# A fused attention and MLP kernel: two heads per load in the first batches, weight requests moved by a slot, small operations moved from VectorE to GpSimd, four more units kept for the end, the last tile in two halves

## The chip, the core and the metric

The kernel runs on one core of a Trainium2 chip. The core has a matrix engine (TensorE, PE in the profile, its weight loads PEld), VectorE (DVE), ScalarE (ACT), GpSimd (POOL) and a fifth engine, SyncE (SP), which here only issues DMA transfers. Each engine runs its instructions in the order in which they are written and waits on semaphores for the others. The metric is the device time in microseconds (us), taken as the median of several runs.

## What is computed

For 8 batches of 8 heads, with 576 positions and 64 dimensions per head, a causal attention with a position bias taken from a running sum of `s`, followed by a layer norm, an MLP of 512 to 2048 to 512 with a relu, and a residual. In short:

```python
scores = scale * q @ k.T                       # per head, 576 x 576
cum = cumsum(max(s, 0))
scores = where(causal, -1e9, scores + min(-(cum[:, None] - cum[None, :]), 0))
attn = softmax(scores)
x = concat_heads(attn @ v)                     # 8 x 576 x 512
xn = (x - mean(x)) / sqrt(var(x) + 1e-6) * g_ln
out = x + relu(xn @ w_ch1) @ w_ch2
```

All inputs and the output are float32 in HBM. The matmuls run in bfloat16.

## The kernel before

**Slots.** The 64 heads are numbered g = 8 * batch + head. The main loop (L714 to L739) has one slot for each. In slot g the score matmuls of head g are issued (`score_mms`), then their exps on ScalarE, then the products with v of head g - 1 (`values`, which ends with a reciprocal and a multiplication into x on VectorE). Around these stand hooks: `at(g, pos, f)` puts a piece of other work at place "a", "a2", "b", "x", "c", "d" or "e" of slot g. The code is scheduled by hand: what is written first is issued first on its engine.

**The bias.** Each head's q and k are extended by four columns with the running sum in three bfloat16 pieces, so that the score matmul adds the bias. `split` (L515 to L522) makes the three pieces with four operations. It runs for batch 0 in the prologue, for batch 1 in slot 2 and for batches 2 to 7 in slot 12. `shift` (L144 to L147) writes the pieces of one batch into the tile `aug` with two operations. `aug` holds q and k of one batch in bfloat16, 128 partitions by 5 row tiles by 16 by 128 columns; the columns from 68 on are padding, which only the DMA transposes of batches 3 and later read. For batches 0 to 2, q and k are transposed by TensorE (`t_quads`, four row tiles and a tail per matrix, copied out of PSUM by VectorE or ScalarE).

**Loads of batches 0 to 2.** These go per head: `head_in` (L422) issues one DMA of 128 KB for a head of q, k or v (512 rows of 64 floats), `tails_in` (L415) one for the last 64 rows of several heads. q and k arrive with four consecutive rows per partition. They land in homes that are reused: k of batch 1 lands where q of batch 0 was, q of batch 2 where k of batch 1 was, and so on, so that a load waits until GpSimd, VectorE or ScalarE have cast the old data to bfloat16 (`cast_head`, from `feed(g)` in slot g for head g + 4). SP issues all of them: batch 0 in the prologue (L460 to L467), batch 1 at the ends of slots 1 and 3, batch 2 in slots 12, 13 and 14 (three, three and two heads). A DMA waits on one of eight semaphores that are used in turn, so SP can have eight transfers under way.

**Weights.** The two weight matrices are requested by GpSimd, which also converts them to bfloat16 on the way: four requests for the up weights (`load_w1`) in slots 7, 7, 8, 8 and four for the down weights (`load_w2`) in slots 9, 9, 10, 10. The first up matmuls stand in slot 11.

**Units.** The MLP of a batch is cut into 32 units of four matmuls each over 512 columns (`chunk_units`: `up` with a relu on ScalarE or VectorE, `down` in quarters, whose last quarter ends with an eviction `yo` on VectorE and a store). The last 64 rows of the batches are gathered in pairs into four further tiles, worked on in two tail chunks of two tiles each, the second of which is the last work of the kernel. The list `units` is worked off inside the slots of the next batch, `nu` units per slot, until KEEP = 10 are left; those are for the end of the batch, where `last_of(b)` computes the last head's values, the layer norm statistics, the normalised `xn` and its transpose, the latter by a DMA for the later batches. Between these steps it works off units. After the loop, the remaining units run one after the other, and their stores are issued by SP.

**Start.** While the first loads are under way, TensorE runs 11 matmuls on the identity matrix whose result nobody reads (`spin(11)`, L493), then the transposes of the running sum (`pq`), which wait for the scan on VectorE. VectorE and GpSimd write a number of constants first (L468 to L481), among them the zero rows under the tails of q, k and v in their homes, and the padding of `aug`: row tile 0 by VectorE, row tiles 1 to 4 by GpSimd at the ends of slots 7 to 10.

Of the kernel before, what the change touches and what calls it, by code (L numbers as in the profile page):

```python
# [9 lines left out]
F32 = mybir.dt.float32  # L10
BF16 = mybir.dt.bfloat16
ALU = mybir.AluOpType
# [4 lines left out]
def kernel(  # L17
# [11 lines left out]
    nc = tc.nc  # L29

    B, H, S, D = q.shape
# [93 lines left out]
    def copy(eng, o, i):  # L125
        if eng == "act":
            nc.scalar.copy(out=o, in_=i)
        elif eng == "dve":
            nc.vector.tensor_copy(out=o, in_=i)  # L129
        else:  # L130
            nc.gpsimd.tensor_copy(out=o, in_=i)  # L131
# [24 lines left out]


    qkT = {}

    def new_t(b):  # L160
        qkT[b] = tpool.tile([P, HD, SP_], BF16, name="qkT", tag="qkT")
# [3 lines left out]
    def t_quads(b, h, engs):  # L165
        pts = [ps_m.tile([P, 2 * 512], BF16, name="pt", tag="pm") for _ in range(2)]
        tails = pts[1][0:DK, NF * P : NF * P + 2 * P].rearrange("r (j n) -> r j n", j=2)
        for i in range(2):
            for p in range(NF):
                nc.tensor.transpose(  # L170
                    pts[i][0:DK, p * P : (p + 1) * P], aug[:, p, i * H + h, 0:DK], ident
                )
# [6 lines left out]
        copy(  # L179
            engs[2],  # L180
            qkT[b][0:DK, :, NF * P : S].rearrange("r (j h) n -> r j h n", j=2)[:, :, h, :],
            tails[:, :, 0:TL],
        )

    def t_dma(b, p):
        nc.sync.dma_start_transpose(
# [168 lines left out]
    def chunk_units(c):  # L355
        st = {}
        na = 2 if c >= B else 4
        per = 4 // na
        tok = na * P

        def up(u):
            if u == 0:
                st["h"] = hpool.tile([P, FB, tok], BF16, name="hT", tag="hT")
            ph = ps_m.tile([P, 512], F32, name="ph", tag="pm")
            for j in range(per):
                fb = u * per + j
                for kd in range(KD):
                    nc.tensor.matmul(  # L368
                        ph[:, j * tok : (j + 1) * tok], lhsT=w1_bf[:, kd, fb * P : (fb + 1) * P],
                        rhs=xnT[c][:, :, kd, :], start=(kd == 0), stop=(kd == KD - 1),  # L370
                    )
            o = st["h"][:, u * per : (u + 1) * per, :].rearrange("p f t -> p (f t)")
            relu(u, o, ph)

        def down(a, qr):
            if qr == 0:
                st["py"] = ps_m.tile([P, 512], F32, name="py", tag="pm")
            for fb in range(4 * qr, 4 * qr + 4):
                nc.tensor.matmul(  # L379
                    st["py"], lhsT=st["h"][:, fb, a * P : (a + 1) * P], rhs=w2_bf[:, fb, :],  # L380
                    start=(fb == 0), stop=(fb == FB - 1),
                )
            if qr == 3:
                yo = ypool.tile([P, Dm], F32, name="yo", tag="yo")
                nc.vector.scalar_tensor_tensor(  # L385
                    out=yo, in0=st["py"], scalar=rstds[c][:, a : a + 1], in1=x_of(c, a),
                    op0=ALU.mult, op1=ALU.add,
                )
                store(c, a, yo)

        for u in range(FB // per):
            units.append(lambda u=u: up(u))
        for a in range(na):
            for qr in range(4):
                units.append(lambda a=a, qr=qr: down(a, qr))

    def mlp(n, eng=None):
        for _ in range(min(n, len(units))):
            stores(eng or nc.scalar, 0 if eng else 1)
            units.pop(0)()  # L400
# [18 lines left out]
            in_=src[what][b, hs, NF * P : S, :].rearrange("h s d -> s h d"),  # L419
        )  # L420

    def head_in(what, b, h, eng):  # L422
        o, i = homes[what, b][:, h, 0:NF, :], src[what][b, h, 0 : NF * P, :]
        if b in QUADS and what != "v":
            eng.dma_start(  # L425
                out=o.rearrange("p t d -> p (t d)"), in_=i.rearrange("(p t) d -> p (t d)", t=NF)
            )
        else:
            eng.dma_start(out=o, in_=i.rearrange("(t p) d -> p t d", p=P))  # L429

    def cast_head(what, b, h, eng):
        i = homes[what, b][:, h, :, :]
# [82 lines left out]
    def split(lo, hi, eng, a=None, o=None):  # L515
        r = r8[:, :, lo:hi]
        a = c8[:, :, lo:hi] if a is None else a
        o = cumh[:, :, lo:hi, :] if o is None else o
        eng.tensor_copy(out=o[:, :, :, 0], in_=a)
        eng.tensor_tensor(out=r, in0=a, in1=o[:, :, :, 0], op=ALU.subtract)  # L520
        eng.tensor_copy(out=o[:, :, :, 1], in_=r)
        eng.tensor_tensor(out=o[:, :, :, 2], in0=r, in1=o[:, :, :, 1], op=ALU.subtract)  # L522
# [36 lines left out]
    def at(g, pos, f):  # L559
        hooks.setdefault((g, pos), []).append(f)  # L560
# [13 lines left out]
    def t_next(g):  # L574
        t_quads(
            (g + 2) // H, (g + 2) % H,
            ("act" if g in(9,10) else "dve", "act" if g >= H else "dve", "dve"),
        )
# [16 lines left out]
    def heads_in(b, hs):  # L595
        for h in hs:
            for what in "qkv":
                head_in(what, b, h, nc.sync)

    def b1_in(h):  # L600
        heads_in(1, (h,))
# [112 lines left out]
    for g in range(NG + 4):  # L714

        nu = n_units.get(g, 0 if g < H else 4)
        if 2 * H <= g < NG:
            nu = max(0, -((KEEP - len(units)) // (H - g % H)))
        run(g, "a")
        if g >= 3:  # L720
            loads()
        if g < NG:
            score_tail = score_mms(g)
            run(g, "a2")
            score_tail()
            score_exp(g, 0)
        mlp(min(1, nu))
# [44 lines left out]
```

The softmax here doesn't subtract the row's maximum and nothing guards it: scores larger than these inputs give would overflow.

## Time and profile before

| | |
|---|---|
| median of 11 runs | 373.03 us (371.65 to 374.45) |
| the profiled execution | 373.2 us |
| its span, first to last instruction | 371.4 us |
| granted TensorE clock, mean | 0.997 |
| HBM read / written | 36.85 MB / 9.44 MB |

The profile is of one execution. It lists the busy time of each engine, the time from the start of the span at which each instruction ran, what an engine had waited for when it started after a pause (in brackets, with the pause in us), and the chain of work that ended last. L numbers are lines of the kernel before. Matmuls are pipelined: a matmul of 512 columns is shown as 379 ns, but 8 of them in a row take 1.73 us. Some matmul records are missing, which shows as short pauses in their place. Where each engine's time is summed over a stretch, the five pairs of numbers are busy us and instructions of PE, PEld, DVE, ACT and POOL; then come the granted TensorE clock, the mean busy share of the 16 DMA engines (it can be above 1, where packets overlap) and GB/s.

The DMA engines are busy for nine tenths or more in most slices of the first 90 us and less than half as much near the end. In the first 75 us the loads of the first three batches and all weights arrive: the eight weight requests are at 28.16, 28.95, 32.11, 32.84, 39.65, 40.47, 46.84 and 47.65 us.

### The profile page before, as it was taken

What the parts mean: (1) busy time and instruction counts of PE and PEld (TensorE: products, weight loads), DVE (VectorE), ACT (ScalarE), POOL (GpSimd) and SP (SyncE); (2) the same over time, 40 slices, a digit from 0 to 9 for tenths busy, and PEclk for the clock granted to TensorE, in tenths of its full rate; (3) what the DMA queues carried; (4) which work ended last, traced back from release to release, by engine and by line L of the source; (5) the groups of instructions that cost most, each with busy time, mean ns of one, the idle gap of its engine ahead of it and who ended that gap; (6) DMA issues with size and microseconds to landing.
All of it is one profiled execution on the core that took longest, in us unless ns stands there. A gap on an engine that the chain in (4) does not pass through costs nothing.

```text
span 371.4 us, 7843 instructions
## 1 busy us (share of the span) xinstructions
PE 351.4 (95%) x2955; PEld 200.6 (54%) x2981; DVE 202.7 (55%) x472; ACT 164.7 (44%) x298; POOL 168.7 (45%) x331
## 2 busy tenths in 40 slices
PE   6997989898999999999999999999999999899994
PEld 2876655564554555555556655455555555344471
DVE  6899585754457345674447335823563454933231
ACT  2767854354542566246524446335634562031020
POOL 5669764855445445484446534654443112500000
PEclk9999999999999999999999999999999999999998
DMA  8979999995998599989999999599404001520202
GB/s 184 232 196 187 215 206 234 230 243 124 208 213 216 131 201 213 224 167 217 196 251 186 222 243 199 76 246 201 100 33 110 31 2 56 116 56 0 86 28 56
DMA packets 168997, 58.86 MB, mean 158 GB/s; under 512 B 154048, under 2 KB 164288, under 8 KB 168960
## 3 DMA queue, kind: packets, MB, share of 16 engines
q1 hardware_dynamic: 158912, 46.17, 62.1%
q0 software_dynamic: 4256, 4.20, 6.8%
q10 hardware_dynamic: 5792, 8.00, 6.7%
q8 instruction: 23, 0.38, 0.4%
q14 instruction: 14, 0.11, 0.1%
HBM read 36.85 MB, written 9.44 MB: 125 GB/s over the span
## 4 chain that ended last, share of the span: by engine, by line
PE 71%; DVE 6%; DMA 3%; SPq 3%; POOL 2%; issue 1%; DVEq 0%; POOLq 0%
PE ph L368 30%; PE py L379 27%; PE s L207 8%; PE pot L258 6%; DVE xn L318 1%; DMA ring<-in_q_dram 1%; POOL aug L131 1%; DMA xnT<-xn 1%; DVE stats L303 1%; SPq L120 1%; SPq L425 1%; DMA x<-in_v_dram 1%; DVE x L267 1%; DVE yo L385 1%; SPq L429 0%
## 5 line engine op out<-in xcount | busy, mean ns | idle before, releaser
L227 ACT ACTIVATE e<-s 128x1024 bf16<-128x1024 f32 (+1 forms) x128 | 99.1, 808 | 85.3 <-PE s L207 85.3
L379 PE MATMUL py<-w_bf,hT 128*128 128x512 bf16 x550 | 129.8, 379 | 1.4
L368 PE MATMUL ph<-xnT,w_bf 128*128 128x512 bf16 x512 | 120.7, 379 | 1.9 <-DMA xnT<-xn 1.8
L230 POOL TENSOR_SCALAR_AFFINE_SELECT e<-e 128x384 bf16<-128x384 bf16 x104 | 45.7, 464 | 111.3 <-ACT e L227 102.7
L353 DVE TENSOR_SCALAR hT<-ph 128x512 bf16<-128x512 f32 x72 | 49.6, 691 | 76.5 <-PE ph L368 75.9
L368 PEld LDWEIGHTS <-w_bf 128*128 128x128 bf16 x640 | 58.2, 98 | 50.5 <-DMA xnT<-xn 2.3
L379 PEld LDWEIGHTS <-hT 128*128 128x128 bf16 x576 | 53.1, 98 | 56.0
L351 ACT ACTIVATE hT<-ph 128x512 bf16<-128x512 f32 x72 | 43.0, 597 | 79.3 <-PE ph L368 78.7
L207 PE MATMUL s<-qkT 68*128 68x192 bf16 (+5 forms) x368 | 55.4, 277 | 0.8 <-DVE qkT L129 0.8
L207 PEld LDWEIGHTS <-qkT 68*128 68x128 bf16 x432 | 36.8, 97 | 31.0 <-DVE x L267 3.0
L385 DVE SCALAR_TENSOR_TENSOR yo<-py,rstd,x 128x512 f32<-128x512 f32 x32 | 24.0, 749 | 47.6 <-PE py L379 45.4
L131 POOL CAST aug<-ring 128x512 bf16<-128x512 f32 (+2 forms) x85 | 44.7, 553 | 6.6 <-DMA ring<-in_k_dram 3.7
L258 PEld LDWEIGHTS <-e 128*128 128x128 bf16 x960 | 37.1, 98 | 12.4 <-POOL e L230 0.8
L258 PE MATMUL pot<-v_bf,e 128*128 128x65 bf16 x960 | 39.7, 193 | 0.6 <-POOL e L230 0.6
L267 DVE TENSOR_TENSOR x<-pot,rinv 128x320 f32<-128x320 f32 x64 | 31.5, 492 | 2.5 <-DMA ring<-in_q_dram 0.2
L129 DVE COPY qkT<-pt 68x512 bf16<-68x512 bf16 (+1 forms) x54 | 24.2, 482 | 8.5 <-PE pt L170 5.0
L303 DVE BATCH_NORM_STATS2 stats<-x 128x6 f32<-128x256 f32 (+2 forms) x68 | 23.4, 399 | 0.3
L318 DVE SCALAR_TENSOR_TENSOR xn<-x,mv,gln_b 128x512 bf16<-128x512 f32 x32 | 22.6, 748 | 0.0
L131 POOL CAST v_bf<-ring 128x512 bf16<-128x512 f32 (+2 forms) x33 | 18.2, 575 | 3.8 <-DMA ring<-in_v_dram 3.8
L266 DVE RECIPROCAL rinv<-pot 128x5 f32<-128x5 f32 x64 | 12.0, 187 | 14.6 <-PE pot L258 14.4
L324 POOL TENSOR_TENSOR rstd<-rstd,nhalf 128x2 f32<-128x2 f32 x18 | 18.9, 1052 | 1.5
L170 PE MATMUL pt<-ident,aug 128*68 128x128 bf16 x192 | 16.4, 219 | 2.9 <-DVE qkT L129 1.4
(78 smaller groups left out, 200.2 us busy)
## 6 DMA issues: line engine op xcount, KB each, us to landing
out_dram<-yo ACTq DMA_DIRECT2D x27, 256.0 KB, 3.4
ring<-in_q_dram SPq DMA_DIRECT2D x20, 256.0 KB, 4.3
ring<-in_k_dram SPq DMA_DIRECT2D x20, 256.0 KB, 4.9
ring<-in_v_dram SPq DMA_DIRECT2D x20, 256.0 KB, 4.2
w_bf<-in_moe_w_ch_dram POOLq DMA_DIRECT2D x8, 512.0 KB, 10.2
ring<-in_k_dram SPq DMA_DIRECT2D x30, 128.0 KB, 3.2
ring<-in_q_dram SPq DMA_DIRECT2D x22, 128.0 KB, 4.0
x<-in_v_dram SPq DMA_DIRECT2D x17, 128.0 KB, 3.6
```

Of the source, the lines that this page charges most:

```text
L131: nc.gpsimd.tensor_copy(out=o, in_=i)
L207: nc.tensor.matmul(d, lhsT=lhsT, rhs=qkT[b][0:DK, h, c0:c1], start=True, stop=not m)
L227: nc.scalar.activation(out=o, in_=i, func=ACT.Exp, scale=scale)
L230: nc.gpsimd.affine_select(out=d, in_=d, compare_op=ALU.is_ge, fill=0.0, base=0, pattern=[[0, d.shape[1]], [1, P]], channel_multiplier=-1,)
L258: nc.tensor.matmul(pot[:, t * D1 : (t + 1) * D1], lhsT=e[:, c : c + P], rhs=v_bfs[b % 2][:, kb, h, :], start=(kb == 0), stop=(kb == t),)
L267: nc.vector.tensor_tensor(out=xs[b][:, :, h * D : (h + 1) * D], in0=pv[:, :, 0:D], in1=rv.to_broadcast([P, NT, D]), op=ALU.mult,)
L303: nc.vector.bn_stats(out=sts[c, a][:, part, :], in_=x_of(c, a)[:, lo:hi])
L351: nc.scalar.activation(out=o, in_=i, func=ACT.Relu)
L353: nc.vector.tensor_scalar_max(out=o, in0=i, scalar1=0.0)
L368: nc.tensor.matmul(ph[:, j * tok : (j + 1) * tok], lhsT=w1_bf[:, kd, fb * P : (fb + 1) * P], rhs=xnT[c][:, :, kd, :], start=(kd == 0), sto ...
L379: nc.tensor.matmul(st["py"], lhsT=st["h"][:, fb, a * P : (a + 1) * P], rhs=w2_bf[:, fb, :], start=(fb == 0), stop=(fb == FB - 1),)
L385: nc.vector.scalar_tensor_tensor(out=yo, in0=st["py"], scalar=rstds[c][:, a : a + 1], in1=x_of(c, a), op0=ALU.mult, op1=ALU.add,)
```

## The change

- `head_in` gets a count `n`. For q and k it loads n heads with one DMA; for v it still issues one DMA per head. In batch 0 heads 0 and 1 are loaded one by one and the rest in pairs. Batches 1 and 2 are loaded in pairs: batch 1 still in slots 1 and 3, batch 2 in slots 11 to 14, one pair in each, where it was slots 12 to 14.
- The two calls of `split` in slots 2 and 12 and the `shift` of batch 1 in slot 5 go from VectorE to GpSimd.
- `load_w1` is called in slots 8, 8, 9, 9.
- The zero rows of v's home of batch 0 are written by VectorE instead of GpSimd, those of q's home of batch 1 by GpSimd in slot 1 instead of before the first loads. The padding of row tile 0 of `aug` is written by GpSimd instead of VectorE; the five GpSimd writes are at the ends of slots 7 to 11.
- `spin(11)` becomes `spin(9)`.
- In the last batch's slots 14 units are kept instead of 10.
- The last tile's 16 down matmuls of 512 columns become two groups of 16 with 256 columns, in two PSUM tiles, each with its own eviction. Each half is stored by two DMAs, one issued by SP and one by ScalarE.
- `t_quads` gets a way to put its third copy behind an exp ("act later"), which no call uses.

```diff
-    def head_in(what, b, h, eng):
-        o, i = homes[what, b][:, h, 0:NF, :], src[what][b, h, 0 : NF * P, :]
-        if b in QUADS and what != "v":
+    def head_in(what, b, h, eng, n=1):
+        if what != "v":
             eng.dma_start(
-                out=o.rearrange("p t d -> p (t d)"), in_=i.rearrange("(p t) d -> p (t d)", t=NF)
+                out=homes[what, b][:, h : h + n, 0:NF, :].rearrange("p h t d -> p h (t d)"),
+                in_=src[what][b, h : h + n, 0 : NF * P, :].rearrange("h (p t) d -> p h (t d)", t=NF),
             )
...
-    for h in range(H + 1):
-        if h < H:
-            head_in("q", 0, h, nc.sync)
-            head_in("k", 0, h, nc.sync)
-        if h:
-            head_in("v", 0, h - 1, nc.sync)
+    for h in (0, 1):
+        for what in "qk":
+            head_in(what, 0, h, nc.sync)
+    head_in("v", 0, 0, nc.sync, 1)
+    for h in range(2, H, 2):
+        for what in "qk":
+            head_in(what, 0, h, nc.sync, 2)
+        head_in("v", 0, h - 1, nc.sync, 2)
+    head_in("v", 0, H - 1, nc.sync)
...
-    for what, eng in zip("qkv", (nc.vector, nc.vector, nc.gpsimd)):
-        eng.memset(homes[what, 0][TL:P, :, NF, :], 0.0)
-    nc.gpsimd.memset(homes["q", 1][TL:P, :, NF, :], 0.0)
-    nc.vector.memset(aug[:, 0, :, DK:P], 0.0)
+    for what in "qkv":
+        nc.vector.memset(homes[what, 0][TL:P, :, NF, :], 0.0)
...
-    spin(11)
+    spin(9)
...
-    at(2, "c", lambda: split(H, 2 * H, nc.vector))
-    at(12, "c", lambda: split(2 * H, BH, nc.vector))
-    at(5, "b", lambda: shift(1, nc.vector))
+    at(2, "c", lambda: split(H, 2 * H, nc.gpsimd))
+    at(12, "c", lambda: split(2 * H, BH, nc.gpsimd))
+    at(5, "b", lambda: shift(1, nc.gpsimd))
...
-    for c, g in enumerate((7, 7, 8, 8)):
+    for c, g in enumerate((8,8,9,9)):
         at(g, "a", lambda c=c: load_w1(c))
...
-    for h, g in enumerate((1, 1, 1, 1, 3, 3, 3, 3)):
+    for h, g in zip(range(0, H, 2), (1, 1, 3, 3)):
         at(g, "e", lambda h=h: b1_in(h))
...
-    for p in (1, 2, 3, 4):
-        at(6 + p, "e", lambda p=p: nc.gpsimd.memset(aug[:, p, :, DK:P], 0.0))
-    B2 = 12
+    at(1, "b", lambda: nc.gpsimd.memset(homes["q", 1][TL:P, :, NF, :], 0.0))
+    for p in range(NT):
+        at(7 + p, "e", lambda p=p: nc.gpsimd.memset(aug[:, p, :, DK:P], 0.0))
+    B2 = 11
...
-        heads_in(2, range(3 * (g - B2), min(H, 3 * (g - B2) + 3)))
-    for g in (B2, B2 + 1, B2 + 2):
+        heads_in(2, 2 * (g - B2))
+    for g in range(B2, B2 + HH):
         at(g, "a", lambda g=g: b2_in(g))
...
-            nu = max(0, -((KEEP - len(units)) // (H - g % H)))
+            keep = 14 if g >= NG - H else KEEP
+            nu = max(0, -((keep - len(units)) // (H - g % H)))
```

The function for the last tile, called in place of the last `down` of the second tail chunk:

```python
def last(a):
    yo = ypool.tile([P, Dm], F32, name="yo", tag="yo")
    for j, (lo, hi) in enumerate(((0, 256), (256, Dm))):
        py = st["py"] if j == 0 else ps_m.tile([P, 512], F32, name="py", tag="pm")
        for fb in range(FB):
            nc.tensor.matmul(
                py[:, lo:hi], lhsT=st["h"][:, fb, a * P : (a + 1) * P],
                rhs=w2_bf[:, fb, lo:hi], start=(fb == 0), stop=(fb == FB - 1),
            )
        nc.vector.scalar_tensor_tensor(
            out=yo[:, lo:hi], in0=py[:, lo:hi], scalar=rstds[c][:, a : a + 1],
            in1=x_of(c, a)[:, lo:hi], op0=ALU.mult, op1=ALU.add,
        )
        for i, eng in enumerate((nc.sync, nc.scalar)):
            eng.dma_start(
                out=out[B - 2 + i, NF * P : S, lo:hi], in_=yo[i * TL : (i + 1) * TL, lo:hi]
            )
```

More of the change, by code (lines that the diff above doesn't have):

```diff
@@ L158 @@
     qkT = {}
+    behind_exp = []
     def new_t(b):
@@ L178, in t_quads @@
             )
[L179 to L183, printed above, removed]
+        o = qkT[b][0:DK, :, NF * P : S].rearrange("r (j h) n -> r j h n", j=2)[:, :, h, :]
+        if engs[2] == "act later":
+            behind_exp.append(
+                lambda: [copy("act", o[:, i, :], tails[:, i, 0:TL]) for i in range(2)]
+            )
+        else:
+            copy(engs[2], o, tails[:, :, 0:TL])
     def t_dma(b, p):
@@ L373, in up @@
             relu(u, o, ph)
+        def last(a):
+            yo = ypool.tile([P, Dm], F32, name="yo", tag="yo")
+            for j, (lo, hi) in enumerate(((0, 256), (256, Dm))):
+                py = st["py"] if j == 0 else ps_m.tile([P, 512], F32, name="py", tag="pm")
+                for fb in range(FB):
+                    nc.tensor.matmul(
+                        py[:, lo:hi], lhsT=st["h"][:, fb, a * P : (a + 1) * P],
+                        rhs=w2_bf[:, fb, lo:hi], start=(fb == 0), stop=(fb == FB - 1),
+                    )
+                nc.vector.scalar_tensor_tensor(
+                    out=yo[:, lo:hi], in0=py[:, lo:hi], scalar=rstds[c][:, a : a + 1],
+                    in1=x_of(c, a)[:, lo:hi], op0=ALU.mult, op1=ALU.add,
+                )
+                for i, eng in enumerate((nc.sync, nc.scalar)):
+                    eng.dma_start(
+                        out=out[B - 2 + i, NF * P : S, lo:hi], in_=yo[i * TL : (i + 1) * TL, lo:hi]
+                    )
         def down(a, qr):
@@ L377, in down @@
                 st["py"] = ps_m.tile([P, 512], F32, name="py", tag="pm")
+            if (c, a) == (B + 1, 1):
+                return last(a) if qr == 3 else None
             for fb in range(4 * qr, 4 * qr + 4):
@@ L420, in tails_in @@
         )
-    def head_in(what, b, h, eng):
-        o, i = homes[what, b][:, h, 0:NF, :], src[what][b, h, 0 : NF * P, :]
-        if b in QUADS and what != "v":
+    def head_in(what, b, h, eng, n=1):
+        if what != "v":
             eng.dma_start(
-                out=o.rearrange("p t d -> p (t d)"), in_=i.rearrange("(p t) d -> p (t d)", t=NF)
-            )
-        else:
-            eng.dma_start(out=o, in_=i.rearrange("(t p) d -> p t d", p=P))
+                out=homes[what, b][:, h : h + n, 0:NF, :].rearrange("p h t d -> p h (t d)"),
+                in_=src[what][b, h : h + n, 0 : NF * P, :].rearrange("h (p t) d -> p h (t d)", t=NF),
+            )
+        else:
+            for j in range(h, h + n):
+                eng.dma_start(
+                    out=homes[what, b][:, j, 0:NF, :],
+                    in_=v[b, j, 0 : NF * P, :].rearrange("(t p) d -> p t d", p=P),
+                )
     def cast_head(what, b, h, eng):
@@ L576, in t_next @@
             (g + 2) // H, (g + 2) % H,
-            ("act" if g in(9,10) else "dve", "act" if g >= H else "dve", "dve"),
+            (
+                "act" if g in (9, 10) else "dve",
+                "act" if g >= H else "dve",
+                "dve",
+            ),
         )
@@ L591, with heads_in @@
             at(g, "a2" if g < H else "b", lambda g=g: t_next(g))
-    for c, g in enumerate((7, 7, 8, 8)):
+    for c, g in enumerate((8,8,9,9)):
         at(g, "a", lambda c=c: load_w1(c))
[L595 to L598, printed above, removed]
+    def heads_in(b, h):
+        for what in "qkv":
+            head_in(what, b, h, nc.sync, 2)
     def b1_in(h):
-        heads_in(1, (h,))
+        heads_in(1, h)
         if h % HH == 0:
@@ L726 @@
             score_exp(g, 0)
+            while behind_exp:
+                behind_exp.pop(0)()
         mlp(min(1, nu))
```

## The prediction

> **What bounds the kernel now.** I read the page's busy table first, then the stretches, then the chain of waits, and last the order of time of the engines wherever the chain leaves TensorE.
>
> ```profile
> PE 351.4 (95%) x2955; PEld 200.6 (54%) x2981; DVE 202.7 (55%) x472; ACT 164.7 (44%) x298; POOL 168.7 (45%) x331
> ```
>
> ```profile
> 15.00:40.00 25.00, 21.86 (x387) 18.85 (x385) 23.56 (x69) 18.79 (x36) 19.39 (x37) 1.00 0.92 196
> 40.00:54.00 14.00, 12.40 (x129) 7.58 (x127) 8.58 (x19) 9.22 (x17) 9.99 (x19) 1.00 1.21 212
> ```
>
> TensorE is busy for 95% of the span, so nothing done on another engine counts unless TensorE stands still for it. The columns of the stretches are PE, PEld, DVE, ACT, POOL. From 15 to 40 us VectorE is busy 23.56 of 25.00: there it is the bound. From 40 to 54 us TensorE loses 1.60 us and the DMA engines are full (1.21). These rows of TensorE's order of time show who stops it (the idle is counted from the modelled end of the matmul before; from issue to issue each hole is some 0.16 longer):
>
> ```profile
> 29.35 0.20 PE L207 MATMUL pot<-qkT 68*128 68x64 bf16 x1 [0.87 <-DVE x L267]
> ...
> 36.86 0.20 PE L207 MATMUL pot<-qkT 68*128 68x64 bf16 x1 [0.88 <-DVE x L267]
> ...
> 51.79 0.38 PE L170 MATMUL pt<-ident,aug 128*68 128x128 bf16 x4 [0.85 <-DVE hT L353]
> ...
> 53.14 0.72 PE L258 MATMUL pot<-v_bf,e 128*128 128x65 bf16 x15 [0.63 <-POOL e L230]
> ```
>
> Before 23.4 us TensorE runs on without such a hole from about 12 us; between 23.4 and 40.5 its holes add up, from issue to issue, to 4.7 us (the other rows: 0.39 at 23.92, 0.45 at 31.39, 0.27 at 33.82, 0.21 at 38.77). Later, up to 86 us, there are some 3.5 us of holes in the transposes of batches 1 and 2, which wait for copies out of PSUM. From there to 322 us only 1.3 us are lost (118 to 120 us, at the PE transposes of batch 2). Then the end of the chain:
>
> ```profile
> 313.75 0.48 PE pot L258 x15
> ...
> 317.39 0.66 DVE yo L385
> ...
> 320.30 4.31 DMA xnT<-xn
> 324.61 0.05 issue
> 324.65 13.99 PE ph L368 x64
> ...
> 359.71 6.65 PE py L379 x30
> 366.36 0.03 issue
> 366.39 0.75 DVE yo L385
> ```
>
> After the last attention head (313.75) the 10 kept MLP units last until about 322.5 (10 x 0.865 = 8.65 us, 8 matmuls being 1.73), while the last batch's x is normalised and transposed by DMA until 324.61. TensorE stands 2.0 us. At the very end the last yo takes 0.75, then SP issues two stores one after the other, each 2.3 us to landing, and the span ends 5.05 us after the last matmul.
>
> **The change, part by part** (against the profiled execution: span 371.4, 373.2 with what lies around it; the median of 11 runs is 373.03, so a change of the one is taken for the other).
>
> *14 units kept in the last batch.* Four units move from heads 56 to 63 to behind the last head. The last head ends 4 x 0.865 = 3.46 us sooner; from there the chain to the transpose's landing takes 324.61 - 314.23 = 10.4 us, and 14 units cover 12.1. The DVE eviction inside that chain (0.66 at 317.39) stays one. The hole goes whole: **-2.0**. What it costs: four slots have three units, not four. Slots of three units stand in the trace at 131 to 145 us with no hole, so nothing. Next late would be the tail's transpose, issued 323.68 and landed long before its matmuls at 352.
>
> *Last tile in two halves.* 16 matmuls of 512 (0.2155 each) become 32 of 256; 64 of that width take 6.99 us here, 0.109 each: +0.05. The first half's eviction and stores lie beside the second half's 1.75 us. The last eviction is 256 wide: an estimate between 0.38 (half of 0.75) and 0.49 (128x320 of L267), I take 0.45: -0.30. SP and ACT issue one store each instead of two on SP: the second one no longer waits 0.52: -0.52. The stores carry half the bytes: -0.1 to -0.2, as 128 KB lands in 2.3. Sum **-0.9** (-0.7 to -1.1).
>
> *Split and shift from DVE to POOL.* DVE loses these, with the four small ones at 17.96 to 19.28 (1.32) and the shift at 25.11 (0.2 of advance):
>
> ```profile
> 48.68 0.85 DVE L519 CAST cumh<-xt 128x240 bf16<-128x240 f32 x1
> 49.57 0.49 DVE L520 TENSOR_TENSOR xt<-xt,cumh 128x240 f32<-128x240 f32 x1
> 50.10 0.53 DVE L521 CAST cumh<-xt 128x240 bf16<-128x240 f32 x1
> 50.66 0.56 DVE L522 TENSOR_TENSOR cumh<-xt,cumh 128x240 bf16<-128x240 f32 x1
> ```
>
> Early pair: DVE is 1.5 us lighter, but TensorE was dense until 23.4, so DVE cannot run ahead of it; following the copies, x and stats from there by hand, x of head 5 ends at about 28.4 instead of 29.3, and this 0.9 is kept because DVE stays dense until 39. **-0.9**; bounds +0.3 (the shift, now behind POOL's casts at 24.5, is what the transposes of slot 6 wait for) and -2.0. At 48.7 the four operations (2.4 us) stand before the relu that frees the buffer for the transposes at 51.79: that 1.0 us hole goes.
>
> They cost time on POOL. No POOL row has a two-input operation of this size; its casts of 128x320 take 0.45, as DVE's do (0.47). The Trainium skill ("GPSIMD Engine Reference", section 4.1 Engine selection) speaks against the move: two-input elementwise work is some 2x slower on GpSimd, one-input work about equal. By the rows the late split takes 2.4 us on POOL, by the rule an estimate of 3.5. I take 3: behind it in POOL's queue are the masks of head 13, on which values(13) wait.
>
> *Pairs, up weights a slot later, B2 = 11, memsets.* From 9.6 to 16.5 us SP issues without a pause, 0.5 us each; six fewer issues per batch, and the DMA engines, at 0.66 to 0.88 between 15 and 30 us, get fed. Bytes and their pieces stay. q and k of heads 2 and 3 land 0.4 to 0.9 us later than alone, k of head 2 at about 9.8 (8.9 before), its transposes run at 11.5: nothing. Batch 1 no longer shares the DMA engines with the up weights, and POOL's two stalls go:
>
> ```profile
> 46.44 0.45 POOL L131 CAST v_bf<-ring 128x320 bf16<-128x320 f32 x1 [2.08 <-DMA ring<-in_v_dram]
> ...
> 52.14 0.47 POOL L131 CAST v_bf<-ring 128x320 bf16<-128x320 f32 x1 [1.76 <-DMA ring<-in_v_dram]
> 52.56 1.72 POOL L230 TENSOR_SCALAR_AFFINE_SELECT e<-e 128x384 bf16<-128x384 bf16 x4
> ```
>
> These held the masks of head 12 until 52.56, hence the 0.63 at 53.14. But POOL's own queue takes their place. From the memset of head 8's slot, which ends at about 36.5, it has: three feeds of casts (1.6, 1.6, 1.2), six weight requests (0.77 each), rstd 1.0, three memsets (0.9 each), a mask pair (0.9): 13.6 us without contention, 14.5 with what the casts at 37.4 show. The masks of head 12 end at 50 to 51; TensorE, 1.9 earlier, wants them at 49.5. A wait of 0.3 to 1.5 replaces 1.8 of holes: **-0.8** (+0.5 to -1.8). The first up chunk is requested at about 30.3; landings of w_bf took 6.8 / 10.2 / 13.2 (minimum, median, maximum) with batch 1 beside them. It is wanted at 39.5: 9.2 us. Alone with the queue emptied I take it near the minimum: nothing. The extra memsets at 15 and 48 us are in the sums above. Batch 2's requests follow the casts of head 15 on POOL, at some 48.5 instead of 50.4; its first use (62.9) waits for other things as well: nothing.
>
> *Spin of 9.* The 11 end at 5.43 and the pq transposes wait for DVE's scan, until 5.87: no gain. The first seven weight loads are spaced 0.43, the later ones 0.21. The skill ("TensorE: Matmul & The Clock Gate", Part 1) says that full speed needs about 3.4 us of activity and that the moment varies. Here it came 2.7 us after the first. By the row the shorter spin costs nothing: the idle before pq becomes about 0.9, and after a hole of that size (at 8.5 us) matmuls went on at full rate. By the rule, where the window falls badly, some 20 matmuls of 128 columns up to 9.4 us run at half rate, 20 x 0.055 = 1.1 us. I take the row.
>
> **Sum.** -2.0 - 0.9 - 0.9 - 0.8 = -4.6. Profiled time 368.6, median 373.03 - 4.6 = **368.4**; its own range is 366.9 to 369.6.
>
> **Rivals.** *Only the end is gained* (0.27): POOL or the DMA engines become the bound from 25 to 54 us and give the early gains back. For it: POOL is busy 9.99 of 14 between 40 and 54 even with its stalls, and gets some 4.5 us more (shift, split, a memset). Against: it loses 3.8 us of waits. 373.03 - 2.9 = 370.1. *All early holes close* (0.15): 23.4 to 40 us loses 2.0, both holes at 51 to 53 us go (1.8): with the end, 373.03 - 6.7 = 366.3. For it: DVE 23.56 of 25; against: POOL's queue above. *Slower* (0.06): POOL's queue in slots 9 to 13. If the casts keep to the 0.66 and 0.91 seen at 37.4 (1.5 and 2 times the usual) and everything on POOL slows by half, its 17 us to the masks of head 13 become 25, they end at about 62 instead of 54 and values(13), wanted at 54.5, hold TensorE 7.5 us: 373.03 - 2.9 - 0.9 + 7.5 = 376.7. It decides from masks later than 54.5 + 3.8 = 58.3. *It doesn't do what it says* (0.06): the last batch's transpose lands as much later after the last head as the kept units last longer, and the early gains are nil; then only the last tile is left, 373.03 - 0.9 = 372.1. Against: nothing in that chain depends on the number of units, and slots of three units have no hole.
>
> **How the numbers follow.** 0.46 for the sum, the rest as given. Faster by over 0.2% (0.75 us, about what a measurement of this kernel tells from no change): the first three cases and a third of the last, 0.90; within: the rest of it, 0.04; slower: 0.06. The range takes in the bounds of the unknown costs and the first two rivals, 366.0 to 371.2.
>
> **What would show it.** No wait on xnT near 320 us; last matmul to end of span about 4.1 instead of 5.05; the holes at x L267 between 28 and 37 us smaller by 0.9 in all; no hT wait near 50 us, and a hole before the values of head 12 that names POOL e. Wrong: up matmuls that wait for w_bf near 40 us, transposes waiting for POOL aug near 49 us, or the first scores later than 9.4.

## The result, and the profile after

| | before | after |
|---|---|---|
| median of the runs | 373.48 us (47 runs, 371.65 to 375.41) | 370.85 us (12 runs, 369.64 to 372.21) |
| the profiled execution | 373.2 us | 371.13 us |
| its span | 371.4 us | 369.0 us |
| last matmul to end of span | 5.04 us | 3.84 us |

The ratio is 0.9928 with an interval of 0.9913 to 0.9944: faster by 2.6 us, where 4.6 were forecast. The busy line of the page and the stretches after the change (here and below, columns and units are those of the part before the prediction):

```profile
PE 353.4 (96%) x2969; PEld 203.9 (55%) x2995; DVE 199.5 (54%) x463; ACT 164.3 (45%) x298; POOL 171.9 (47%) x341
```

```profile
15.00:40.00 25.00, 22.27 (x408) 19.57 (x406) 23.78 (x67) 19.06 (x37) 18.76 (x41) 1.00 0.91 197
40.00:54.00 14.00, 13.88 (x145) 8.71 (x143) 7.12 (x19) 10.36 (x20) 13.69 (x24) 1.00 1.01 156
```

From 40 to 54 us TensorE is now busy for 13.88 of 14.00 (12.40 before): the holes are gone. VectorE is still full from 15 to 40. GpSimd is busy for 13.69 of 14.00 between 40 and 54, so it works without a pause, and still nobody on TensorE waits for it there. What the busy line cannot tell is where 3.6 us were lost again. For that the start of one fixed instruction in each slot, the score matmul of the last row tile, was taken in both traces; the table gives after minus before, and its steps are the account of the change:

| place | after minus before | step |
|---|---|---|
| slot 0 (11.84 us before) | +1.65 | **+1.65** the start |
| slot 3 | +1.57 | |
| slots 7 to 13 | +0.70 | **-0.9** at slots 4 to 6 |
| slot 14 (55.22 us before) | -1.21 | **-1.9** both holes at 51 to 53 us |
| slots 18 to 60 | +0.74 | **+2.0** between slots 15 and 16 |
| down matmuls of the last tiles (359.44 us before) | -1.24 | **-2.0** the kept units |
| end of the span | -2.4 | **-1.2** the last tile |

Two losses that the sum did not have are in it: a late start, and a wait for batch 2's loads. The first is in TensorE's order of time at the start; before, and then after:

```profile
6.50 0.61 PE L487 MATMUL idle<-ident 128*128 128x512 bf16 x2
7.41 0.41 PE L170 MATMUL pt<-ident,aug 128*68 128x128 bf16 x4 [0.30 <-ACT aug L528]
```

```profile
6.49 1.03 PE L517 MATMUL idle<-ident 128*128 128x512 bf16 x2
7.39 0.64 PE L171 MATMUL pt<-ident,aug 128*68 128x128 bf16 x4
```

The columns are the start and the busy time of a group. The work starts at the same moment, and the matmuls last up to twice as long: two spins of 512 columns that stand later 1.03 us and not 0.61, four transposes 0.64 and not 0.41. From 9 to 14 us, in the view by stretches (PE, PEld, DVE, ACT, POOL, the clock, the DMA share, GB/s), first before, then after:

```profile
9.00:14.00 5.00, 4.32 (x72) 3.88 (x73) 3.99 (x9) 3.28 (x7) 3.71 (x9) 1.00 1.05 254
```

```profile
9.00:14.00 5.00, 4.33 (x40) 3.97 (x40) 2.98 (x6) 2.09 (x5) 3.47 (x9) 1.00 1.21 271
```

In the same 4.3 busy us TensorE does 40 instructions and not 72. The clock column says 1.00 in both, and the mean granted clock after is 1.000. Both mislead here, because the trace's record of the clock has its first entry, to full rate, only at 13.8 us (4.3 us before), and what lies ahead of the first entry counts as full. The rate must be read from the spacing of equal matmuls.

The second loss is in the chain of waits of after (start, length, what), which leaves TensorE at 52 us:

```profile
52.58 11.24 DMA ring<-in_q_dram
66.08 0.75 DVE stats L306 x2
```

q of batch 2's first two heads is issued at 52.58 and is usable at 63.9. VectorE, which casts it, stands for 2.13 us, then does its casts, and everything queued behind them, the norm of batch 1 among it, is late. TensorE waits for that at its transposes. The cast before, the cast after, and TensorE's wait after:

```profile
62.93 0.87 DVE L129 CAST aug<-ring 128x320 bf16<-128x320 f32 x2
```

```profile
63.94 0.88 DVE L129 CAST aug<-ring 128x320 bf16<-128x320 f32 x2 [2.13 <-DMA ring<-in_q_dram]
```

```profile
67.78 0.40 PE L338 MATMUL ptx<-ident,xn 128*128 128x128 bf16 x4 [1.05 <-DVE xn L321]
```

Before, that cast ran with no wait for a DMA. Why the load is late is shown by the DMA columns of the stretches (share, then GB/s, at the end of the rows), first before, then after:

```profile
38.00:40.00 2.00, 1.79 (x31) 1.56 (x27) 1.31 (x4) 2.00 (x5) 2.00 (x5) 1.00 1.22 212
40.00:42.00 2.00, 1.88 (x16) 0.96 (x14) 0.00 (x0) 1.82 (x3) 1.84 (x4) 1.00 1.21 242
```

```profile
38.00:40.00 2.00, 1.79 (x40) 1.68 (x38) 1.97 (x5) 2.00 (x5) 2.00 (x5) 1.00 0.17 31
40.00:42.00 2.00, 1.88 (x21) 1.24 (x19) 0.04 (x1) 2.00 (x4) 2.00 (x4) 1.00 0.04 7
```

For four us the DMA engines have next to nothing to do. GpSimd issues the first two up weights at 30.68 and 31.54 and gets to the third only at 40.34 (32.11 before). Between them stands other work of its queue, which first waits for VectorE and then runs on to the request:

```profile
34.52 0.61 POOL L276 COPY xt<-x 64x512 f32<-64x512 f32 x1 [2.23 <-DVE x L270]
...
40.34 1.59 POOL L150 DMA_DIRECT2D w_bf<-in_moe_w_ch_dram  x2
```

Batch 1 is in, batch 2 is not due. The third to the eighth request then land between 45.9 and 62.2 us (42.5 to 59.1 before) and share the engines with batch 2's loads.

The end is near the forecast. The chain of after, where the last of the kept units begin:

```profile
314.14 9.44 PE py L403 x43
323.59 13.81 PE ph L371 x64
...
361.65 3.51 PE py L384 x32
365.16 0.03 issue
365.19 0.48 DVE yo L388
```

There is no DMA piece between py and ph any more: the kept units reach to 323.59, and the up matmuls of the last batch start in the same moment. The last eviction takes 0.48, and the span ends 3.84 after the last matmul.

### The profile page after: what moved, and what is told of

It reads as the page before. It is cut to its first block, busy times and chain, and to the rows that moved or that the text cites. A ratio compares the mean times of both kernels' runs of the same rounds, so it can differ in the third digit from the quotient of the medians.

```text
span 369.0 us, 7841 instructions
## 1 busy us (share of the span) xinstructions
PE 353.4 (96%) x2969; PEld 203.9 (55%) x2995; DVE 199.5 (54%) x463; ACT 164.3 (45%) x298; POOL 171.9 (47%) x341
## 4 chain that ended last, share of the span: by engine, by line
PE 81%; DVE 7%; POOL 4%; DMA 4%; issue 2%; ACT 0%; SPq 0%; DVEq 0%; POOLq 0%
PE ph L371 30%; PE py L403 30%; PE s L210 10%; PE pot L261 6%; DMA ring<-in_q_dram 3%; PE pt L171 2%; DVE qkT L129 2%; DVE stats L306 2%; DVE x L270 1%; DVE xn L321 1%; PE py L384 1%; POOL aug L673 1%; POOL aug L131 1%; DMA x<-in_s_dram 1%; POOL w_bf L155 1%
## 5 line engine op out<-in xcount | busy, mean ns | idle before, releaser
L403 PE MATMUL py<-w_bf,hT 128*128 128x512 bf16 x534 | 126.3, 379 | 1.4
L403 PEld LDWEIGHTS <-hT 128*128 128x128 bf16 x560 | 51.5, 98 | 54.8 <-DVE hT L356 0.4
L210 PE MATMUL s<-qkT 68*128 68x192 bf16 (+5 forms) x368 | 56.3, 280 | 0.8 <-DVE qkT L129 0.8
L171 PE MATMUL pt<-ident,aug 128*68 128x128 bf16 x192 | 17.8, 231 | 1.4 <-DVE qkT L129 1.3
```

The lines of the kernel that those rows point to most:

```text
L210: nc.tensor.matmul(d, lhsT=lhsT, rhs=qkT[b][0:DK, h, c0:c1], start=True, stop=not m)
L403: nc.tensor.matmul(st["py"], lhsT=st["h"][:, fb, a * P : (a + 1) * P], rhs=w2_bf[:, fb, :], start=(fb == 0), stop=(fb == FB - 1),)
```

## The experiments

"The changed kernel" is the kernel after. For the first experiments the theory was that the two losses are separate, the one from the spins, the other from the moment at which the up weights are requested. Where two variants are compared, the difference of their ratios is given with the root of the summed squares of the half intervals.

**Eleven spins in the changed kernel.**

```diff
-    spin(9)
+    spin(11)
```

> The changed kernel with 11 spin matmuls again. Theory (with 9 spins TensorE does not reach its full rate before the first scores and runs at half rate to about 14 us): the first scores of head 1 come about 1.6 us sooner than in the changed kernel, the time goes from 370.85 to about 369.3-369.9 (ratio to before 0.988 to 0.990). Rival (the paired loads make the start late): the start stays 1.6 us late and the ratio stays at 0.993. Second rival (the moment at which full rate comes is chance, not the count of spins): the profile may show either, and the median moves by less than 0.5 us.

369.24 us, ratio 0.9896 [0.9867, 0.9925]; below the changed kernel by 0.0032, give or take 0.0033. In its trace the full rate is there from 4.55 us, slot 0 stands at -0.13, and a step of +1.3 between slots 15 and 16 remains (+2.0 in the changed kernel). The same transposes as above take 0.41 again:

```profile
7.29 0.41 PE L171 MATMUL pt<-ident,aug 128*68 128x128 bf16 x4 [0.30 <-ACT aug L558]
```

The paired loads are still in place, so they are not what makes the start late. The loss at the start is what the theory said; by medians alone it would be at the edge.

**Nine spins in the kernel before.**

> The kernel before with 9 spin matmuls and nothing else. Theory (half rate to about 14 us): slower by 0.7 to 1.6 us, ratio 1.002 to 1.004, of which a part may be hidden where VectorE is the bound from 16 to 40 us; the profile shows 128-column matmuls spaced 0.107 us between 8 and 14 us. Rival (pairs make the start late): ratio 1.000.

373.92 us, ratio 1.0010 [0.9994, 1.0026]. The loss of 0.7 to 1.6 us that was expected does not show in time. The trace shows a loss at the start of 2.4 us (+2.44 at slots 5 to 13) and then +0.93 from slot 14 on. So in this trace the kernel before hides 1.5 us of a late start in the holes at 51 to 53 us: the wait for GpSimd's masks, which hung on a load of v, is gone, and the wait for hT is 0.24 instead of 0.85. The changed kernel has lost that cover.

**The up weights back in slots 7, 7, 8, 8.**

```diff
-    for c, g in enumerate((8,8,9,9)):
+    for c, g in enumerate((7, 7, 8, 8)):
```

> The changed kernel with the up weights requested in slots 7, 7, 8, 8 again. Theory (the weights asked for a slot later leave the DMA engines idle near 40 us and push the down weights into batch 2's loads, so that q and k of its heads 0 and 1 land 2 us late): q of head 0/1 of batch 2 lands before 62, the pause before the transposes at 66.6 us (1.2 us, VectorE's xn) goes, and the time falls by 1.0 to 2.0 us, to about 369-370 (ratio 0.988 to 0.990). Rival (the pairs themselves are late, both heads having to arrive): q and k of heads 0 and 1 of batch 2 still land at 63 to 65 and the ratio stays at 0.993. Second rival: batch 1's loads again share the DMA engines with the weights, GpSimd's casts wait for v of its last heads, and 1 us is lost near 50 us.

369.39 us, ratio 0.9879 [0.9855, 0.9904]; 0.0049 below the changed kernel, give or take 0.0029. Lateness is -0.64 at slot 14 and -0.64 at slot 16: the step of +2.0 is gone, and the -1.9 at slot 14 stays. q of batch 2's first pair lands at 62.0 instead of 63.8, and its cast does not wait:

```profile
62.29 0.87 DVE L129 CAST aug<-ring 128x320 bf16<-128x320 f32 x2
```

The pairs are still in place, so the rival, that a load is late because it waits for two heads, is out. The later request bought nothing: the holes at 51 to 53 us go without it too.

**14 kept units in the kernel before.**

```diff
-            nu = max(0, -((KEEP - len(units)) // (H - g % H)))
+            keep = 14 if g >= NG - H else KEEP
+            nu = max(0, -((keep - len(units)) // (H - g % H)))
```

> The kernel before with 14 instead of 10 units kept in the last batch. Theory: the 2.0 us hole before the last batch's up matmuls goes and nothing else changes: -2.0 us, ratio 0.9946. Rival (slots of three units have holes, or the transpose lands later): ratio 0.998 to 1.000.

371.62 us, ratio 0.9951 [0.9929, 0.9973], so -1.8 us. In the chain of its trace, between 311 and 326 us, the last batch's up matmuls follow the kept units without a wait, at 322.81 instead of 324.65:

```profile
310.94 11.87 PE py L379 x55
322.81 3.24 PE ph L368 x15
```

**Both losses undone at once, with eleven and with thirteen spins.**

> The changed kernel with both losses undone at once: eleven spins and the up weights requested in slots 7, 7, 8, 8. Theory (two separate losses, one at the start, one at batch 2's first use): the gains add. Each alone brought about 1.5 us, so against the kernel before -2.6 - 1.5 - 1.5, about -5.5 (range -5.0 to -6.0), a ratio of about 0.985; no lateness at slot 0 and no step at slots 15 and 16. Rival (both losses are hidden behind one common limit, the loads of the first 65 us): what one edit wins the other cannot win again, -4.2, a ratio of 0.989, and a hole near slots 15 and 16 is back.

> As the one before, with thirteen spins. Theory (the moment of full rate varies from run to run, and a longer unbroken start makes the early moment surer): the same median or up to 0.5 us less than with eleven spins, and runs that agree more closely. Rival (eleven were enough, and two more only hold up the transposes of the running sum): 0.2 to 0.5 us more.

Eleven: 367.71 us, 0.9837 [0.9809, 0.9864]. Thirteen: 367.97 us, 0.9832 [0.9811, 0.9854], four runs within 0.3 us. The gains add: some 6 us below before. Which of the two is better can't be told. The eleven's profiled execution had the late start (+1.77 at slot 0) and no step between slots 15 and 16, and its runs show the price: four at 367.5 to 367.7 us with a mean clock of 0.998 or above, two at 369.1 and 370.1 with 0.993 and 0.990. These two kernels are the fastest of the study.

**Thirteen spins in the kernel before.**

> The kernel before with thirteen spin matmuls instead of eleven and nothing else. Theory (the moment of full rate varies from run to run and thirteen in a row make the early one surer): the granted clock of the runs lies at 0.998 or above, and the time is 0.3 to 1.0 us below before, whose runs are mixed. Rival (thirteen only hold up the transposes of the running sum, and before hides a late start anyway near 50 us): no difference or 0.3 more.

373.07 us, ratio 0.9995 [0.9976, 1.0014]: no difference. The theory that a longer spin makes the early moment sure fell: the profiled execution had the late start with thirteen (+2.35 at slot 0, +0.15 from slot 14 on), and the runs' mean clocks go from 0.986 to 1.0 (0.988 to 1.0 in the kernel before). It is confirmed that this kernel hides most of a late start: 2.2 of 2.35 us here, 1.5 of 2.44 in the trace with nine.

**The last tile in two halves, alone.**

> The kernel before with the last tile in two halves and nothing else. Theory: from the last matmul to the end of the span about 4.1 us instead of 5.05, nothing else moves, -0.7 to -1.1 us, a ratio of 0.9970 to 0.9981. Rival (the end is set by the landing of a store, which does not care for size or queue): at most -0.3, no difference.

372.60 us, ratio 0.9978 [0.9966, 0.9990], so -0.8 us. Its last matmul ends at 366.35 (366.36 before) and the span at 370.4 instead of 371.4: 4.05 us where there were 5.04.

**Split and shift back on VectorE in the changed kernel, both, and the late split alone.**

```diff
-    at(12, "c", lambda: split(2 * H, BH, nc.gpsimd))
+    at(12, "c", lambda: split(2 * H, BH, nc.vector))
```

> The changed kernel with split and shift back on VectorE, the rest of the change in place. Theory (the move to GpSimd brought 0.9 in slots 4 to 6, and about 1.0 of the 1.9 us near 51 us, the hole that waited for VectorE's hT): 1.9 us more than the changed kernel, about 372.8; the step of -0.9 at slots 4 to 6 is missing, and a wait on hT near 50 us is back. Rival (the holes near 51 us went because batch 1 is loaded earlier, whatever engine splits): only 0.9 more, about 371.8.

> The changed kernel with only the late split (slot 12) back on VectorE. Theory (a cast from float32 to bfloat16 on VectorE stands still while GpSimd works without a pause; in the changed kernel GpSimd has its later memsets there): the first cast of the split takes about 2.3 us as with all of split and shift on VectorE, TensorE waits 2.9 us for hT, and the time is about 2.6 us above the changed kernel, near 373.5; the step of -0.9 at slots 4 to 6 stays. Rival (the long cast comes from the early split's delay and VectorE's lateness): the cast takes 0.9, the hole 1.0, and the time is 0.9 above the changed kernel.

Both: 374.42 us, ratio 1.0016 [1.0001, 1.0031], 0.0088 above the changed kernel (give or take 0.0022), 3.3 us where 1.9 were expected. The late split alone: 372.99 us, 0.9991 [0.9977, 1.0005], 2.4 us above. The early part is the rest, 0.9, give or take 0.8. In the traces the step at slots 4 to 6 is -0.4 with both on VectorE, where the expectation had none, and -0.9 with the late split alone. Why the late part is worth more than the 1.0 us hole of the kernel before is in VectorE's and GpSimd's order of time of the run with the late split on VectorE, and in TensorE's:

```profile
49.93 2.29 DVE L549 CAST cumh<-xt 128x240 bf16<-128x240 f32 x1
...
49.84 0.48 POOL L131 CAST aug<-x 128x320 bf16<-128x320 f32 x1
50.23 0.52 POOL L131 CAST aug<-ring 128x320 bf16<-128x320 f32 x1
50.71 0.46 POOL L131 CAST v_bf<-ring 128x320 bf16<-128x320 f32 x1
51.11 0.89 POOL L673 MEMSET aug<- 128x960 bf16 x1
51.96 2.04 POOL L233 TENSOR_SCALAR_AFFINE_SELECT e<-e 128x384 bf16<-128x384 bf16 x4
```

```profile
54.99 0.38 PE L171 MATMUL pt<-ident,aug 128*68 128x128 bf16 x4 [2.80 <-DVE hT L356]
```

VectorE's first cast took 0.85 in the kernel before and takes 2.29 here. It starts 0.09 us after a cast of GpSimd, and it ends 0.2 after the last of four GpSimd instructions, three casts and a memset, that follow each other without a pause. In the kernel before GpSimd had only a memset and two casts there, and then stood still, waiting for a load of v (1.76 us). TensorE pays with 2.80 us.

In both of these traces there is a second price. One us after the long hole TensorE falls to half rate for 3.41 us (from 56.05 us in this trace). Five score matmuls, which take 0.82 us in the next run below, take 1.48:

```profile
57.65 1.48 PE L210 MATMUL s<-qkT 68*128 68x512 bf16 x5
```

How many runs pay it, their mean clocks do not tell for sure: in the changed kernel five of twelve have 1.000, with the late split on VectorE none has more than 0.995. So the 2.4 us hold the hole and, in a part of the runs at least, the half rate behind it.

**The same with the last two writes of the padding out of the way.**

```diff
-        at(7 + p, "e", lambda p=p: nc.gpsimd.memset(aug[:, p, :, DK:P], 0.0))
+        at(7 + p if p < 3 else 14 + p, "e", lambda p=p: nc.gpsimd.memset(aug[:, p, :, DK:P], 0.0))
```

> As the one before, and the last two writes of the padding, 0.9 us each on GpSimd, in slots 17 and 18 instead of 10 and 11. Theory (the cast stands still for as long as GpSimd has work without a pause): with 1.8 us less of it in front, the first cast takes 0.5 to 1.4 us instead of 2.3, the hole at hT 1.0 to 2.0 instead of 2.9, and the time is 0.9 to 1.9 us below the run before. Rival (the cast's length has nothing to do with GpSimd, it is the DMA engines' traffic into the same memory): the cast keeps 2.3, the hole 2.9, the time stays.

370.95 us, ratio 0.9929 [0.9906, 0.9953]: 0.0062 below the run before (give or take 0.0027), and level with the changed kernel, with the late split on VectorE. Its rows:

```profile
51.96 0.38 PE L171 MATMUL pt<-ident,aug 128*68 128x128 bf16 x4 [0.61 <-DVE hT L356]
...
53.83 0.82 PE L210 MATMUL s<-qkT 68*128 68x512 bf16 x5
```

```profile
49.08 0.61 DVE L549 CAST cumh<-xt 128x240 bf16<-128x240 f32 x1
...
48.95 0.49 POOL L131 CAST v_bf<-ring 128x320 bf16<-128x320 f32 x1
49.37 1.15 POOL L233 TENSOR_SCALAR_AFFINE_SELECT e<-e 128x384 bf16<-128x384 bf16 x2
```

With only one cast of GpSimd to wait for, VectorE's takes 0.61, and TensorE's hole is 0.77 from issue to issue instead of 2.96. That is more than the 0.9 to 1.9 us expected, because the half rate goes with the long hole. The rival, the traffic of the DMA engines, for which the cast would have kept its 2.3, is out: their share is 1.21 between 49 and 52.2 us in the run before and 1.19 here.

The Trainium skill ("SBUF — State Buffer", section "SBUF: two separate sides") says that VectorE, in a fast mode that uses both its ports, and GpSimd take a shared pair of ports as an exclusive lock, held for a whole instruction, and that the loser waits. Whether the cast runs in that mode, no run here shows. The traces agree so far that the cast takes 0.39 us where GpSimd does nothing (kernel before with thirteen spins), and 2.29 and 2.27 in the two runs above. They do not show who gets the next turn. With 14 units kept in the kernel before, VectorE's cast ended 0.3 us after the first of two GpSimd casts without a pause between them, while the second was running, and did not wait for both:

```profile
49.26 0.68 DVE L519 CAST cumh<-xt 128x240 bf16<-128x240 f32 x1
...
49.20 0.47 POOL L131 CAST aug<-x 128x320 bf16<-128x320 f32 x1
49.59 0.57 POOL L131 CAST aug<-ring 128x320 bf16<-128x320 f32 x1
```

GpSimd's masks slow a cast without stopping it: the second cast of the split, 0.41 us alone, takes 0.95 beside three of them.

**Split and shift on GpSimd in the kernel before.**

> The kernel before with split and shift on GpSimd and nothing else. Theory (as above, and the wait of the values of head 12 on GpSimd's masks belongs to the late loads of batch 1's v): -0.9 at slots 4 to 6; at 51 us the hT hole goes, while the masks of heads 12 and 13, behind the stalled casts and the split on GpSimd, hold TensorE as long or longer: in all -0.5 to -1.9, a ratio of 0.995 to 0.9987. Rival (VectorE's relief alone closes both holes): -2.8, a ratio of 0.9925.

373.47 us, ratio 1.0001 [0.9974, 1.0028]: inconclusive in time, with single runs from 371.8 to 378.0 us. The gain is below the rival's 2.8 in any case (its 0.9925 lies outside the interval); of the 0.5 to 1.9 expected, the interval leaves at most 1.0. The profiled execution had a late start (+1.50 at slot 0), then -1.0 up to slot 7 and -0.7 at slot 14. The hT hole is gone, and this stands in its place:

```profile
52.96 0.72 PE L258 MATMUL pot<-v_bf,e 128*128 128x65 bf16 x15 [0.95 <-POOL e L230]
```

So in the kernel before, with its late loads of v, VectorE's relief brings 0.7 us near 51 us, where the changed kernel has 1.9: GpSimd's masks take the rest. They stand behind a cast of v that waits for its load until 51.95 us; in the changed kernel no cast of v waits there. That the earlier loads are what lets the changed kernel have both is read from these rows and not tested alone.

## Why the prediction was right in its direction, and too large by two us

| step of the prediction | predicted | measured | by |
|---|---|---|---|
| 14 units kept | -2.0 | -2.0 | trace; alone -1.8 |
| last tile in two halves | -0.9 | -1.2 | trace; alone -1.0 in its trace, -0.8 by medians |
| early split and shift to GpSimd | -0.9 | -0.9 | trace; 0.9, give or take 0.8, by the two runs with VectorE |
| holes at 51 to 53 us | -0.8 | -1.9 | trace |
| spin of 9 | 0 | +1.65 | trace; -1.2 by medians when undone |
| batch 2's first use | 0 | +2.0 | trace; -1.8 by medians when undone |
| sum | -4.6 | -2.4 | span; -2.6 by medians |

That 2.6 of the 4.6 us came is in part luck: two losses of 3.6 us in all were put at nothing in the sum, and 1.4 us of gains beyond it made up for a part of them.

**Right.** The kept units and the last tile came out to within 0.3 us by their own working: ten units did not cover a chain of 10.4 us, fourteen do; the second store no longer waits on SP. The early split came out in size, but not by its working. The four holes at x L267 were to shrink and did not; they stand at 30.05, 32.08, 34.51 and 37.55 us with the pauses of before (0.87, 0.45, 0.27 and 0.88). What went lies in slots 4 to 6, mainly the 0.39 at 23.92, and 0.4 of it went with VectorE too.

**Failed: the spin.** "By the row the shorter spin costs nothing", and then "I take the row". The rule of the skill that stood beside it gave 1.1 us, and 1.65 was measured. The sign that the prediction had named, first scores later than 9.4 us, came: they start at 9.67. The row was one execution in which the full rate happened to come at 4.3 us. A moment that varies from run to run can't be priced from a single trace, and the sum stood on a lucky one.

**Failed: the request a slot later.** The sum checked the first up chunk, which indeed came in time, and said of batch 2 that "its first use (62.9) waits for other things as well: nothing". That was looked at as an order of issue and not as bytes. The weights' 4 MB were moved from a stretch in which batch 1's loads stood beside them to one in which batch 2's do; GpSimd's queue delayed the second pair of requests not by some 2.5 us, as the first, but by 8 (32.11 to 40.34), 2.2 of them a wait for VectorE, and the DMA engines ran dry before it. The kernel with only this undone has no such step.

**Mis-sized: the holes at 51 to 53 us.** "A wait of 0.3 to 1.5 replaces 1.8 of holes": no wait replaced them. The masks of head 12 began at 51.34, later than the text's 50 to 51 for their end, but TensorE was 0.7 late at slot 13 and asked for them later. The late start is not the reason, though: with eleven spins in the changed kernel TensorE was 1.0 early at slot 13, the masks began at 49.67, the values followed at 50.34, and no wait stood there either. What the text had too early is the moment at which TensorE asks. By its own rows the values of head 12 could start at 52.51 (53.14 less the wait of 0.63); 1.9 earlier is 50.6, and not 49.5. With masks that end at 50 to 51 the wait is then 0.4 at most. The late split took 2.7 us on GpSimd with its gaps, near the 3 taken. Its two-input operations took 0.64 and 0.70, where VectorE takes 0.41 and 0.56 with nothing of GpSimd's beside it, so 1.25 to 1.6 times as long, which is less than the skill's factor of two. And a cost of leaving the split where it was, VectorE held up by GpSimd and TensorE's half rate after the hole, was nowhere in the working: with the other parts of the change, it would have been 2.4 us.

A smaller slip: pairs save six issues in batch 0, as the text says, but eight in batches 1 and 2.

**Rivals.** Of the four, "only the end is gained" names a time (370.1) close to the measured one, but not the cause: neither GpSimd's masks nor a full DMA gave the early gains back, but a late start and DMA engines left idle. The slower one, masks behind GpSimd's queue, did not come near its point of decision: the masks behind the late split started at 54.88, against 58.3.

**Open.** What decides when the full rate comes is not fully known. In all fourteen traces the record of the clock changes only in steps of 3.41 us, and where these steps lie against the start of the span differs from execution to execution. With nine spins all six traces start late: in four the full rate came at 4.9 to 5.9 us and went again one step later, in two it first came at 13.3 and 13.8. With eleven or thirteen, five of eight had it from 4.3 to 7.3 us on, and three lost it again. The runs' mean clocks point the same way for the kernel before: 0.990 or less, as in its trace with nine spins (0.989), in 14 of 22 runs with nine, in 4 of 28 with eleven beside them, and in 2 of 22 with thirteen. So fewer spins make the late start likelier, and no number that was tried makes the early one sure. By medians, eleven or thirteen are better than nine in the changed kernel by about 1.2 to 1.6 us (two pairs of kernels, 0.0032 give or take 0.0033 and 0.0042 give or take 0.0037). No run takes back the pairs, the earlier batch 2 or the moved writes of zeros alone.

## What to carry to other kernels

A hole that closes also stops covering what was late before it: in the kernel before, 1.5 us of a late start vanished at 51 us, after the change it reaches the end. When a transfer is moved, lay out the bytes of all transfers of the stretch with the moment that its issuing engine's queue lets it go, and look for idle DMA engines; the first user of the moved one is often not the one that suffers. Where two engines hold each other up, as VectorE and GpSimd do here, small constants written in a full stretch can be the whole price: two writes of 0.9 us were worth 2.3.

## What the hardware showed that was not expected

- The full rate of TensorE can come, go and come again: with nine spins in the kernel before, full rate was granted from 5.92 to 9.33 us, half rate to 16.16, and then full rate to the end. The page's clock column and mean show nothing of a late start when the record begins only with the change to full rate.
- A hole of 2.80 us in TensorE was followed one us later by half rate for 3.41 us; after holes of 0.6 to 0.95 us at this place, in other traces, it stayed at full rate.
- A cast of 128x240 from float32 to bfloat16 on VectorE, 0.39 to 0.41 us alone, took 0.61 to 0.85 beside two or three GpSimd instructions and 2.29 beside four in a row.
- Two-input operations on 128x240 elements took 0.64 and 0.70 on GpSimd, and 0.41 and 0.56 on VectorE.
